# Attention and two expert stages on one core: x in a score bank's columns, k kept, some steps moved

## The chip, the cores and the metric

One NeuronCore of a Trainium2 chip runs the whole program. The metric is the device time of one execution in microseconds (us); lower is better. PE is the matmul engine (PEld its weight loads), DVE the vector engine, ACT the scalar engine, POOL the GpSimd engine, SP the engine whose queue issues most DMAs.

## What is computed

The input of the first stage is q, k, v of 4 batches, 8 heads, 576 rows, 64 columns, all float32. Three stages follow one another:

```python
scores = q @ k^T / 8                        # per batch and head: 576 x 576
kth    = the 32nd largest score of a row
attn   = softmax over the scores >= kth     # the others count as zero
x      = attn @ v                           # put together: 2304 tokens x 512

h = x @ w_in                                # 512 -> 2048
x = (max(h,0) + alpha*min(h,0)) @ w_out     # 2048 -> 512

skip   = x @ w_skip > 0                     # else the row goes out as it is
expert = argmax(x @ w_gate), p its softmax  # 8 experts
out    = x + p * (relu(x @ w1[e]) @ w2[e])  # 512 -> 1024 -> 512
```

Float32 is reached with fp32r matmuls of a high and a low part: three products for each one. The low part is a value less its rounded copy, made by `sub` on POOL (L108).

## The kernel before

**Units and steps.** The unit of attention is one batch, one pair of heads and one tile of 128 query rows. Rows 512 to 575 of both heads make a mixed unit, half as wide. A batch is two works: first the query tiles 0 and 1 of its four pairs (8 units), then the tiles 2, 3 and the mixed one (12 units). There are 80 units. The main loop makes one step per unit, and a step has 14 slots. The list `STEP` says which part of which unit is issued in which slot; `(1, -2, "values")` means: in slot 1, for the unit two steps back. So parts of five units (-2 to 2) are in work at a time, and each engine runs its own instructions in the order in which they were issued.

**A unit's course.** `scores` (PE, L417 and L411) fills four banks of PSUM, `copy` (ACT, L422) brings them to SBUF as `sb`. A step later `fold` (DVE, L438) halves the row by maxima and minima three times; four `round`s find the 32 largest values (MAX8 L447, MATCH_REPLACE8 L450). `exp` (ACT, L472) and `weights` (DVE, L480: compare with the 32nd value, multiply, sum) make the weights, `recip` and `spread` their sum's reciprocal. `turn` (PE, L510 to L516) transposes them, `evac` (ACT, L522 to L533) copies them to `PT` and the reciprocals to `R`. `values` (PE, L539 and L543) multiplies with v, `out` (DVE, L550; ACT, L552; POOL through `sub`) writes the high and the low part of x.

**Heads.** For each pair, `heads` loads q and k, transposes them (PE, L343 and L349) and splits them into parts (`part`: two ACT copies, L330 and L331, and one `sub`). Both works of a batch do that for their own query tiles, and both for all of k. Its pieces are issued by the "heads" entries of `STEP`, for the pair after the current one.

**PSUM.** Eight banks: psS has three (scores, heads, and row tiles at the end), psT two (the fourth score block and transposes 0 and 1 of the weights), psM two (everything of the second and third stages until the end), psX one. psX holds in its two halves, for alternate units, transpose 2 (the tail columns and the reciprocals) and then x of `values`. In the last stage `second` writes its product there too.

**The rest of the work.** Beside attention, a queue `todo` holds the pieces of the second stage (`moe1`: `up` L611, relu L621 to L630, `down` L657, copies L666) with their costs in us; each slot takes as much as its budget allows. Pieces that follow after so many slots go by the list `late`: after the matmuls of an `up` group, `late1` (ACT) runs one slot later, then `LA` slots pass, then `late2` (DVE, L624) reads the bank and frees it; `late3` is POOL's `sub` of g, which `between` holds back from slot 9 on until slot 1 of the next step. At most five or six groups are in this state (`held`). When a work's second stage is done, `rows` issues logits, the routing (`route`, L767 to L776, on DVE), the row tiles (transposed and stored), the ranks (PE, L802 and L803), `slots` (DVE, L812 to L820) and scatters by DMA (POOL, L826).

**The beginning.** In the first 170 us the weights w_in and w_out are converted: 32 loads (SP, L258 and L262), for each three ACT operations (L277 to L281), `bits` (DVE, L285), `split` (POOL, L291 and L108), `store`. `bits` issues the load that stands `AHEAD` places further on.

**The end.** After the last unit the remaining second stage runs, then the experts over blocks of 128 rows (`first` L1015, `second` L1033, `finish` L1041), each beside the splitting of the weights for the next (L986, L987).

`fold` leaves its last instruction in `gate`, and the next `sub` waits for it:

```python
gate[0] = nc.vector.tensor_tensor(o[:, n_], a[:, n_, 0:w], a[:, n_, w:2 * w], op=op)
```

Of the kernel before, what the change touches and what calls it, by code (L numbers as in the profile page):

```python
# [23 lines left out]
STEP = [(0, 0, "exp", 0), (0, 0, "exp", 1), (0, 1, "fold"),  # L24
        (1, -2, "values"), (1, 2, "scores"), (1, 0, "certify"),
        (2, -1, "recip"), (2, 1, "round", 0), (2, 2, "copy", 0),
        (3, 2, "copy", 1),
        (4, 1, "round", 1), (4, 0, "heads", 0),
        (5, -1, "spread"), (5, -1, "turn", 0), (5, 0, "heads", 1),
# [4 lines left out]
        (11, 0, "weights", 1)]  # L34
AHEAD = 3
EC = 32
PH = 9
RD = 3
# [7 lines left out]
CC = 0.5  # L46
LA = 2
CV = 4
HL = 2
# [9 lines left out]
def kernel(  # L59
# [43 lines left out]

    gate, now, held_back = [None], [None], []

# [29 lines left out]

    banks, xbank = [0, 0], [None]

# [17 lines left out]
    def room():  # L155
        return banks[0] - banks[1] < 2
# [78 lines left out]
    wout32 = w_out.bitcast(I32)  # L235
    raws, converted, pads = {}, set(), {}
    todo, late, convq, rowq = [], [], [], []
# [29 lines left out]
    def convert(i):  # L267
# [36 lines left out]

        return none * (CV - 1 if i != 1 else 3 * CV) + [bits] + none * (CV - 1) + [split] + none * CV + [store]


    def heads(b, p, i, us):

        hd = dict(vb=vbd[i], qb=qbd[i])  # L310
        full = [u for u in us if u < SF]
        own = ((full[0], full[-1] + 1), (0, SF))
        nats = {}

        def load():
            tail = att.tile([128, 2, D], F32, name="nat_t", tag="nat_t", bufs=2)
            for s, src in enumerate((q, k)):
                nat = att.tile([128, SF, 2, D], F32, name="nat", tag="nat", bufs=2)
                r0, r1 = own[s]
                for h in range(2):  # L320
                    (nc.scalar if s and quick[0] else nc.sync).dma_start(nat[:, r0:r1, h, :],
                                      src[b, 2 * p + h, 0:SB, :].rearrange("(p r) d -> p r d", p=128)[:, r0:r1])
                (nc.scalar if s and quick[0] else nc.sync).dma_start(tail[s * TL:(s + 1) * TL], src[b, 2 * p:2 * p + 2, SB:S, :].rearrange("h t d -> t h d"))
                nats[s] = nat
            nats[2] = tail
# [8 lines left out]
        def turn(s):  # L334
            if s == 0:

                hd["q"] = att.tile([128, 2, SB], F32R, name="qT", tag="qT", bufs=2)
                hd["k"] = att.tile([128, 2, S + TL], F32R, name="kT", tag="kT", bufs=2)
            r0, r1 = own[s]
            c0, c1 = r0 * 128, r1 * 128  # L340
            pt = htile()[:, c0:c1]
            for r in range(r0, r1):
                nc.tensor.transpose(pt[:, r * 128 - c0:(r + 1) * 128 - c0], nats[s][:, r].rearrange("p h d -> p (h d)"),  # L343
                                    ident)
            late.append((HL, lambda: part(hd["k"][:, :, TL:TL + SB] if s else hd["q"][:, :, c0:c1], pt)))

        def turn_t():
# [3 lines left out]
            def copies():  # L351
                part(hd["k"][:, :, 0:TL], pt[:, TL:128])
                nc.gpsimd.tensor_copy(hd["k"][:, :, S:S + TL], hd["k"][:, :, 0:TL].bitcast(F32))
                if SF not in us:
# [20 lines left out]
        hd["load"] = load  # L375
        return hd, [lambda: turn(0), turn_t, lambda: turn(1)]

# [11 lines left out]
    class Unit:  # L389


        def __init__(self, hd, u, p, getx, col, ai, exact, vi, lastu):
            self.hd, self.u, self.p, self.getx, self.col, self.ai = hd, u, p, getx, col, ai
            self.exact, self.vi, self.lastu = exact, vi, lastu
# [5 lines left out]
        def scores(self):  # L400

            hd, u = self.hd, self.u
            self.sbp, self.sb = padded("sb", 3, 3.0e38)
            self.ps = {}
            for j in range(2):
                for h in range(self.nh):
                    self.ps[h, j] = ptile() if h and j else psS.tile([128, 512], F32, name="ps", tag="ps")
                for i, (a, b_) in enumerate(((0, 0), (1, 0), (0, 1))):
# [5 lines left out]
                    for h in range(2):  # L414
                        gp = slice(h * 64, (h + 1) * 64)
                        c0 = TL * (1 - h) + j * HALF
                        nc.tensor.matmul(self.ps[h, j][:, 0:HALF], lhsT=hd["q"][gp, a, u * 128:(u + 1) * 128],  # L417
                                         rhs=hd["k"][gp, b_, c0:c0 + HALF], **se)
# [74 lines left out]
        def turn(self, h):  # L493
# [5 lines left out]
            if h < 2 and h >= self.nh:  # L499
                return  # L500
            if h < 2:
                pt = ptile()
            else:
                c0 = self.ai % 2 * 256
                pt = xbank[0][:, c0:c0 + 256]
            self.pt[h] = pt
# [28 lines left out]
        def values(self):  # L535
            hd, PT = self.hd, self.PT
            n = 64 if self.mix else 128
            x = self.x = self.pt[2][:, 0:n]
            nc.tensor.matmul(x[:, 0:n], lhsT=hd["vb"], rhs=PT[:, 8, 0:n], start=True, stop=False)  # L539
# [6 lines left out]
        def out(self):  # L546
# [5 lines left out]
            nc.scalar.activation(xh[:, self.p, cols], xf[:, 0:n], AF.Copy)  # L552
            sub(xl[:, self.p, cols], xf[:, 0:n], xh[:, self.p, cols].bitcast(F32))

# [25 lines left out]
    def moe1(xx, cols, x2t, base):  # L580
# [20 lines left out]
        def up(wi, f, sg, half, first):  # L601
# [15 lines left out]

            ra = moe.tile([128, 320], F32, name="ra", tag="ra", bufs=6)[:, 0:n]

# [55 lines left out]
        for hf in range(nhf):  # L675
            for f in range(hf * fs, (hf + 1) * fs):
                for sg, (c0, c1) in enumerate(cols):
                    for half in range(2):
                        one = f % 2 == 0 and sg == 0 and half == 0
                        if half == 0:  # L680
                            parts.append((lambda: room() and held[0] < 6, None))
                        parts.append((6 * (c1 - c0) / 2400, lambda wi=wi, f=f, sg=sg, half=half, one=one:
# [27 lines left out]
    def rows(b, us, colof, x2t, hook, then):  # L710
# [123 lines left out]

        parts = [(lambda: not early[0] and rroom(), None), (0.1, logits)] + [(0, None)] * RD + [(0.1, route)]
        for i in range(nu):
            parts += [(rroom, None), (0.45, lambda i=i: row(i)), (0, None)]
            if i == min(1, nu - 1):
                parts += [(rroom, None), (0.1, ranks)]
# [188 lines left out]
    def second(hs, W):  # L1028
        yp = xtile_()
        i = 0  # L1030
# [74 lines left out]
    def main(work, exact, hooks=(lambda: [], lambda: [])):  # L1105
# [51 lines left out]
        def unit(kx):  # L1157
            if kx not in units:
# [14 lines left out]
                us = work[wi][1]  # L1173
                units[kx] = Unit(hds[pi], u, p, getx, colofs[wi][u], kx, exact, us.index(u), u == us[-1])
            return units[kx]

# [37 lines left out]

        xbank[0] = xtile_()
# [69 lines left out]
        now[0] = None  # L1285
        release(held_back)

    work = []
# [195 lines left out]
```

## Time and profile before

| | us |
|---|---|
| median of 3 runs | 1085.13 (1083.98 to 1085.79) |
| the profiled execution | 1084.56 |
| its span, first to last instruction | 1082.8 |
| PE busy / DVE busy in it | 935.1 / 922.2 |
| ACT busy / POOL busy in it | 703.0 / 429.7 |

The durations come from the one profiled execution, whose span leaves out 1.8 us around it. The mean granted clock of PE is 0.947. In a wait, the idle time of an engine is put down to the instruction that released it last.

### The profile page before, as it was taken

To read this page: it belongs to the slowest core of one execution; us is meant where nothing else is said; L and a number is where in the kernel's file an instruction comes from. 1 tells how busy PE (TensorE), PEld (TensorE's weight loads), DVE (VectorE), ACT (ScalarE), POOL (GpSimd) and SP (SyncE) were. 2 spreads that over 40 slices of the span, in tenths; PEclk is the share of its full clock that TensorE was granted. 3 is DMA by queue.
4 is the path that set the end of the run, shared out by engine and by line. 5 is a ranking of instruction groups with operands and counts; after the bars stand their busy time and mean duration, and the time that the engine had idled before them with its cause. 6 is when DMAs were issued, how large, how long until landed. Compare 5 with 4: busy or idle time off the path is not lost.

```text
span 1082.8 us, 21930 instructions
## 1 busy us (share of the span) xinstructions
PE 935.1 (86%) x7270; PEld 844.8 (78%) x7270; DVE 922.2 (85%) x2943; ACT 703.0 (65%) x1804; POOL 429.7 (40%) x577
## 2 busy tenths in 40 slices
PE   4435668998999989989998998999899998798995
PEld 2224458898998878989998898999789897587884
DVE  4999999999999799999989998999895233899972
ACT  6969857765865576567657766866674343597871
POOL 5766754422542334344224433532341330427221
PEclk9966669998999999999999999999999999899998
DMA  7888985665656566766656666665556798899960
GB/s 218 296 276 214 304 259 184 223 214 172 223 190 229 164 214 195 256 222 225 213 167 215 213 252 224 205 225 195 174 203 235 271 349 340 279 356 397 346 234 15
DMA packets 154282, 254.13 MB, mean 235 GB/s; under 512 B 78062, under 2 KB 110830, under 8 KB 137776
## 3 DMA queue, kind: packets, MB, share of 16 engines
q1 hardware_dynamic: 150464, 247.84, 67.6%
q0 software_dynamic: 2496, 4.50, 1.2%
q8 instruction: 59, 0.97, 0.4%
q14 instruction: 63, 0.52, 0.1%
q10 hardware_dynamic: 1200, 0.30, 0.1%
HBM read 224.20 MB, written 29.71 MB: 234 GB/s over the span
## 4 chain that ended last, share of the span: by engine, by line
PE 41%; DVE 37%; issue 6%; ACT 6%; POOL 5%; DMA 5%; SPq 0%; POOLq 0%; DVEq 0%; ACTq 0%
PE pm L657 14%; DVE v L447 8%; PE pm L611 6%; DVE F L438 5%; DVE Ex L480 5%; DVE m L438 4%; DVE F L450 4%; PE px L1033 4%; PE pm L1015 4%; PE px L543 4%; DVE ra L624 3%; PE ps L417 2%; PE pt L510 2%; POOL cv L108 2%; PE pm L723 1%
## 5 line engine op out<-in xcount | busy, mean ns | idle before, releaser
L611 PE MATMUL pm<-x,wr 128*128 128x256 f32 (+1 forms) x1536 | 248.8, 309 | 17.0 <-DVE ra L624 10.3
L657 PE MATMUL pm<-g,wr 128*128 128x256 f32 (+1 forms) x1536 | 236.0, 304 | 4.1 <-DMA wr<-wout 3.5
L611 PEld LDWEIGHTS pm<-x,wr 128*128 128x128 f32 x1536 | 215.7, 194 | 28.2 <-DVE ra L624 14.8
L657 PEld LDWEIGHTS pm<-g,wr 128*128 128x128 f32 x1536 | 210.2, 190 | 9.9 <-issue 4.1
L447 DVE MAX8 v<-F 128x8 f32<-128x72 f32 (+2 forms) x576 | 212.9, 405 | 0.8
L108 POOL TENSOR_TENSOR g<-ra,g 128x256 fp32r<-128x256 f32 (+1 forms) x128 | 104.9, 824 | 185.8 <-ACT g L630 95.6
L480 DVE SCALAR_TENSOR_TENSOR Ex<-sb,v,Ex 128x577 f32<-128x577 f32 x144 | 129.8, 928 | 0.0
L450 DVE MATCH_REPLACE8 F<-v,F 128x72 f32<-128x72 f32 (+1 forms) x432 | 122.8, 289 | 0.0
L422 ACT ACTIVATE sb<-ps 128x288 f32<-128x288 f32 x224 | 80.0, 411 | 62.2 <-PE ps L417 51.3
L630 ACT ACTIVATE g<-ra 128x256 fp32r<-128x256 f32 (+1 forms) x128 | 57.1, 446 | 75.1 <-DVE ra L624 73.3
L472 ACT ACTIVATE Ex<-sb,st 128x576 f32<-128x576 f32 x144 | 104.7, 775 | 0.1
L522 ACT ACTIVATE PT<-pt 128x512 f32<-128x512 f32 x144 | 86.9, 604 | 16.3 <-PE pt L510 15.6
L624 DVE SCALAR_TENSOR_TENSOR ra<-ra,slope,pm 128x256 f32<-128x256 f32 (+1 forms) x128 | 64.6, 505 | 32.1 <-ACT ra L621 30.2
L543 PE MATMUL px<-PT,vt 128*64 128x128 f32 (+1 forms) x1280 | 89.2, 286 | 0.0
L510 PE MATMUL pt<-ident,Ex 128*128 128x128 f32 x576 | 85.9, 281 | 2.6 <-ACT sb L422 2.6
L108 POOL TENSOR_TENSOR x<-xf,x 128x128 fp32r<-128x128 f32 (+1 forms) x80 | 49.3, 617 | 96.0 <-ACT x L552 94.8
L417 PE MATMUL ps<-kT,qT 64*128 64x288 f32 x576 | 79.5, 348 | 6.1 <-ACT kT L330 2.0
L543 PEld LDWEIGHTS px<-PT,vt 128*64 128x64 f32 x1280 | 70.1, 147 | 9.9 <-issue 1.8
L417 PEld LDWEIGHTS ps<-kT,qT 64*128 64x128 f32 x576 | 61.4, 210 | 19.3 <-issue 9.4
L510 PEld LDWEIGHTS pt<-ident,Ex 128*128 128x128 f32 x576 | 70.7, 146 | 3.9 <-ACT sb L422 3.5
L621 ACT ACTIVATE ra<-pm 128x256 f32<-128x256 f32 (+1 forms) x128 | 52.4, 409 | 30.9 <-PE pm L611 28.7
L438 DVE TENSOR_TENSOR F<-m 128x144 f32<-128x144 f32 (+2 forms) x240 | 70.2, 344 | 0.0
(431 smaller groups left out, 1834.8 us busy)
## 6 DMA issues: line engine op xcount, KB each, us to landing
wr<-win SPq DMA_DIRECT2D x64, 1024.0 KB, 4.9
wr<-wout SPq DMA_DIRECT2D x64, 1024.0 KB, 4.9
wraw<-in_moe_w_dram SPq DMA_DIRECT2D x88, 512.0 KB, 6.3
wr<-in_moe_w_in_dram SPq DMA_DIRECT2D x16, 512.0 KB, 6.1
vt<-in_v_dram SPq DMA_DIRECT2D x32, 256.0 KB, 2.8
win<-cv SPq DMA_DIRECT2D x16, 512.0 KB, 4.8
wr<-in_moe_w_out_dram SPq DMA_DIRECT2D x16, 512.0 KB, 5.6
wout<-cv SPq DMA_DIRECT2D x32, 256.0 KB, 4.1
```

The lines of the kernel that those rows point to most:

```text
L108: i = nc.gpsimd.tensor_tensor(o, a, b, op=OP.subtract)
L417: nc.tensor.matmul(self.ps[h, j][:, 0:HALF], lhsT=hd["q"][gp, a, u * 128:(u + 1) * 128], rhs=hd["k"][gp, b_, c0:c0 + HALF], **se)
L438: gate[0] = nc.vector.tensor_tensor(o[:, n_], a[:, n_, 0:w], a[:, n_, w:2 * w], op=op)
L447: nc.vector.max(v8[:, h, r, :], F[:, h, 0:w])
L450: nc.vector.match_replace(out=F[:, h, 0:w], in_to_replace=v8[:, h, r, :], in_values=F[:, h, 0:w], imm_value=NEG)
L472: nc.scalar.activation(self.Ex[:, h, :], self.sb[:, h, :], AF.Exp, bias=self.st[:, 0, h:h + 1], scale=0.125)
L480: nc.vector.scalar_tensor_tensor(self.Exp[:, cs], self.sbp[:, cs], v8[:, h, 3, 7:8], self.Exp[:, cs], op0=OP.is_ge, op1=OP.mult, accum_out ...
L510: nc.tensor.transpose(pt[:, c * 128:(c + 1) * 128], P[:, c0:c0 + 128], ident)
L543: nc.tensor.matmul(x[h * 64:(h + 1) * 64, 0:n], lhsT=hd["vt"][:, h, c, :], rhs=rhs, start=False, stop=(c == SF - 1))
L611: nc.tensor.matmul(hp[:, 0:n], lhsT=w[:, (f % 2) * 8 + a * 4 + d, :], rhs=x[:, d, c0:c1], start=(i == 0), stop=(i == 3 * KD - 1))
L624: nc.vector.scalar_tensor_tensor(ra, ra, slope[:, f:f + 1], hp[:, 0:n], op0=OP.mult, op1=OP.add)
L657: nc.tensor.matmul(op_[:, 0:n], lhsT=w[:, 2 * f + a, :], rhs=g[(hf + ch) * 8 + f, sg][:, gg, 0:n], start=(i == 0), stop=(i == ni - 1))
```

## The change

- **Kept k.** Only the first work of a batch loads k, transposes it and splits it; the result is kept per pair (four tiles `kT0` to `kT3`), and the second work uses it. q's tile holds two query tiles and not four.
- **Beginning.** Four weight loads are ahead and not three; the fourth is issued behind the second pair's loads. The first conversion's `bits` and `split` come after fewer slots.
- **x in a score bank.** A new part `begin` takes the unit's four score banks. `values` writes x into the columns from 288 on of the bank of the new unit's first head and second half; transpose 2 has psX to itself. Heads' transposes of q and k take banks of psT. `second` takes a bank of psS.
- **Slots.** `values` and `scores` go from slot 1 to slot 2, the copies one slot later each, the first heads entry from slot 4 to slot 3.
- **Low parts.** `sub` of x is kept until slot 1 of the next step (except for a work's last unit). `LA` goes from 2 to 3, with one `ra` buffer less. `route` is issued after the first row tile and three more slots.

The diff, without the parts that only carry these through:

```diff
-        (1, -2, "values"), (1, 2, "scores"), (1, 0, "certify"),
-        (2, -1, "recip"), (2, 1, "round", 0), (2, 2, "copy", 0),
-        (3, 2, "copy", 1),
-        (4, 1, "round", 1), (4, 0, "heads", 0),
+        (1, 0, "certify"),
+        (2, -1, "recip"), (2, 1, "round", 0), (2, 2, "begin"), (2, -2, "values"), (2, 2, "scores"),
+        (3, 2, "copy", 0), (3, 0, "heads", 0),
+        (4, 2, "copy", 1), (4, 1, "round", 1),
...
-AHEAD = 3
+AHEAD = 4
-LA = 2
+LA = 3
...
-        return none * (CV - 1 if i != 1 else 3 * CV) + [bits] + none * (CV - 1) + [split] + none * CV + [store]
+        if i == 0:
+            return none + [bits, split] + none * (2 * CV) + [store]
+        return none * (CV - 1 if i > 1 else 3 * CV) + [bits] + none * (CV - 1) + [split] + none * CV + [store]
...
+        fresh = us[0] == 0
...
+                if s and not fresh:
+                    nc.sync.dma_start(tail[TL:2 * TL], src[b, 2 * p:2 * p + 2, SB:S, :].rearrange("h t d -> t h d"))
+                    continue
...
-                hd["q"] = att.tile([128, 2, SB], F32R, name="qT", tag="qT", bufs=2)
-                hd["k"] = att.tile([128, 2, S + TL], F32R, name="kT", tag="kT", bufs=2)
+                hd["q"], hd["c0"] = att.tile([128, 2, 256], F32R, name="qT", tag="qT", bufs=2), own[0][0] * 128
+                if fresh:
+                    kept[p] = att.tile([128, 2, S + TL], F32R, name="kT", tag=f"kT{p}", bufs=1)
+                hd["k"] = kept[p]
-            pt = htile()[:, c0:c1]
+            pt = ptile()[:, c0:c1]
...
-        return hd, [lambda: turn(0), turn_t, lambda: turn(1)]
+        return hd, [lambda: turn(0), turn_t] + ([lambda: turn(1)] if fresh else [])
...
-                    self.ps[h, j] = ptile() if h and j else psS.tile([128, 512], F32, name="ps", tag="ps")
+                    self.ps[h, j] = ptile() if h and j else htile()
+            spare[0] = self.ps[0, 1]
...
-            if h < 2:
-                pt = ptile()
-            else:
-                c0 = self.ai % 2 * 256
-                pt = xbank[0][:, c0:c0 + 256]
+            pt = ptile() if h < 2 else xtile_()
...
-            x = self.x = self.pt[2][:, 0:n]
+            bank = spare[0] if spare[0] is not None else htile()
+            spare[0] = None
+            x = self.x = bank[:, HALF:HALF + n]
...
-            sub(xl[:, self.p, cols], xf[:, 0:n], xh[:, self.p, cols].bitcast(F32))
+            def low():
+                sub(xl[:, self.p, cols], xf[:, 0:n], xh[:, self.p, cols].bitcast(F32))
+            if self.end or now[0] is None:
+                low()
+            else:
+                held_x.append(low)
...
-            ra = moe.tile([128, 320], F32, name="ra", tag="ra", bufs=6)[:, 0:n]
+            ra = moe.tile([128, 320], F32, name="ra", tag="ra", bufs=5)[:, 0:n]
-                            parts.append((lambda: room() and held[0] < 6, None))
+                            parts.append((lambda: room() and held[0] < 5, None))
...
-        parts = [(lambda: not early[0] and rroom(), None), (0.1, logits)] + [(0, None)] * RD + [(0.1, route)]
+        parts = [(lambda: not early[0] and rroom(), None), (0.1, logits)] + [(0, None)] * RD
         for i in range(nu):
+            if i == 1:
+                parts += [(0, None)] * RD + [(0.1, route)]
             parts += [(rroom, None), (0.45, lambda i=i: row(i)), (0, None)]
...
-        yp = xtile_()
+        yp = htile()
...
-            for i in range(AHEAD):
+            for i in range(AHEAD - 1):
...
+        if not exact:
+            conv_load(*convs[AHEAD - 1])
...
                 if x == 1 or now[0] is None:
                     release(held_back)
+                    release(held_x)
```

## Rows read from the trace of the kernel before

**Rows 1.** The page: engine shares; DVE and clock in 40 slices.

```profile
PE 935.1 (86%) x7270; PEld 844.8 (78%) x7270; DVE 922.2 (85%) x2943; ACT 703.0 (65%) x1804; POOL 429.7 (40%) x577
...
PE   4435668998999989989998998999899998798995
...
DVE  4999999999999799999989998999895233899972
```

**Rows 2.** Stretches of 25 us: busy us per engine, granted clock, DMA share, GB/s.

```profile
225.00:250.00 25.00, 25.00 (x248) 23.74 (x247) 24.83 (x93) 17.02 (x54) 6.55 (x13) 1.00 0.73 250
250.00:275.00 25.00, 21.95 (x167) 20.71 (x166) 22.10 (x95) 15.10 (x44) 7.76 (x14) 0.80 0.50 157
```

**Rows 3.** DVE's waits, 175 to 825 us: total us, times, longest us.

```profile
DVE ra L624 <- ACT ra L621: 8.5, 13, 2.3
DVE rc L767 <- ACT lg L732: 8.3, 3, 3.8
DVE rc L767 <- ACT lg L730: 5.3, 2, 2.7
DVE xf L550 <- PE px L543: 3.6, 3, 1.3
DVE tot L814 <- PE pm L803: 3.1, 4, 1.1
```

**Rows 4.** DVE's waits, 0 to 175 us.

```profile
DVE cv L285 <- ACT cv L281: 14.6, 7, 7.3
DVE ra L624 <- ACT ra L621: 3.5, 2, 2.7
```

**Rows 5.** Timeline, 20 to 30 us: start, us, engine, line, idle before.

```profile
24.38 0.91 DVE L285 SCALAR_TENSOR_TENSOR cv<-cv 128x512 int32<-128x512 int32 x1 [2.67 <-ACT cv L281]
...
27.60 0.67 ACT L277 ACTIVATE cv<-wr 128x512 f32<-128x512 f32 x1 [3.25 <-DMA wr<-in_moe_w_in_dram]
...
29.60 1.13 DVE L285 SCALAR_TENSOR_TENSOR cv<-cv 128x512 int32<-128x512 int32 x1 [0.71 <-ACT cv L281]
```

**Rows 6.** PE's waits, 175 to 825 us.

```profile
PE pm L611 <- DVE ra L624: 10.3, 18, 1.4
PE px L539 <- ACT R L528: 7.6, 6, 1.8
PE px L512 <- DVE xf L550: 6.7, 8, 3.0
...
PE ps L343 <- ACT sb L422: 1.3, 2, 0.9
```

**Rows 7.** Groups by shape, 175 to 825 us: busy us, mean ns, idle before.

```profile
L480 DVE SCALAR_TENSOR_TENSOR Ex<-sb,v,Ex 128x577 f32<-128x577 f32 x121 | 106.2, 904 | 0.0
...
L108 POOL TENSOR_TENSOR x<-xf,x 128x128 fp32r<-128x128 f32 x53 | 34.1, 643 | 61.3 <-ACT x L552 60.8
```

**Rows 8.** Timeline around 519 us.

```profile
519.08 0.80 DVE L480 SCALAR_TENSOR_TENSOR Ex<-sb,v,Ex 128x577 f32<-128x577 f32 x1
...
519.48 0.73 POOL L108 TENSOR_TENSOR x<-xf,x 128x128 fp32r<-128x128 f32 x1 [0.26 <-ACT x L552]
...
519.81 1.02 DVE L480 SCALAR_TENSOR_TENSOR Ex<-sb,v,Ex 128x577 f32<-128x577 f32 x1
```

**Rows 9.** Groups by shape again, 175 to 825 us: k's splitting.

```profile
L330 ACT ACTIVATE kT<-ps 128x512 fp32r<-128x512 f32 x25 | 15.0, 598 | 7.4 <-PE ps L343 7.4
...
L108 POOL TENSOR_TENSOR kT<-raw__6693,kT 128x512 fp32r<-128x512 f32 x1 | 1.3, 1290 | 0.1
```

**Rows 10.** Timeline around 544 us: scores, x's reader, score copies.

```profile
544.07 0.79 PE L417 MATMUL ps<-kT,qT 64*128 64x288 f32 x7
...
544.28 0.29 DVE L550 TENSOR_TENSOR xf<-px,R 128x128 f32<-128x128 f32 x1 [1.25 <-PE px L543]
...
544.77 1.02 ACT L422 ACTIVATE sb<-ps 128x288 f32<-128x288 f32 x3 [1.40 <-PE ps L417]
```

**Rows 11.** PE's waits, 825 to 1083 us.

```profile
PE px L1033 <- DVE orow L1041: 2.3, 1, 2.3
```

More of the change, by code (lines that the diff above doesn't have):

```diff
@@ L102 @@
     ctx.enter_context(tc.manual_schedule())
-    gate, now, held_back = [None], [None], []
+    gate, now, held_back, held_x = [None], [None], [], []
     def sub(o, a, b):
@@ L134, in xtile_ @@
         return psX.tile([128, 512], F32, name="px", tag="px")
-    banks, xbank = [0, 0], [None]
+    banks, spare = [0, 0], [None]
     def mtile():
@@ L235 @@
     wout32 = w_out.bitcast(I32)
-    raws, converted, pads = {}, set(), {}
+    raws, converted, pads, kept = {}, set(), {}, {}
     todo, late, convq, rowq = [], [], [], []
@@ L312, in heads @@
         own = ((full[0], full[-1] + 1), (0, SF))
+        fresh = us[0] == 0
+        assert own[0][1] - own[0][0] <= 2
         nats = {}
@@ L344, in turn @@
                                     ident)
-            late.append((HL, lambda: part(hd["k"][:, :, TL:TL + SB] if s else hd["q"][:, :, c0:c1], pt)))
+            late.append((HL, lambda: part(hd["k"][:, :, TL:TL + SB] if s else hd["q"][:, :, 0:c1 - c0], pt)))
         def turn_t():
@@ L351, in copies @@
             def copies():
-                part(hd["k"][:, :, 0:TL], pt[:, TL:128])
-                nc.gpsimd.tensor_copy(hd["k"][:, :, S:S + TL], hd["k"][:, :, 0:TL].bitcast(F32))
+                if fresh:
+                    part(hd["k"][:, :, 0:TL], pt[:, TL:128])
+                    nc.gpsimd.tensor_copy(hd["k"][:, :, S:S + TL], hd["k"][:, :, 0:TL].bitcast(F32))
                 if SF not in us:
@@ L393, in __init__ @@
             self.hd, self.u, self.p, self.getx, self.col, self.ai = hd, u, p, getx, col, ai
-            self.exact, self.vi, self.lastu = exact, vi, lastu
+            self.exact, self.vi, self.lastu, self.end = exact, vi, lastu, False
             self.mix = u == SF
@@ L398, in __init__, with begin @@
             self.pt = {}
-        def scores(self):
-            hd, u = self.hd, self.u
+        def begin(self):
             self.sbp, self.sb = padded("sb", 3, 3.0e38)
@@ L406, in scores @@
                 for h in range(self.nh):
-                    self.ps[h, j] = ptile() if h and j else psS.tile([128, 512], F32, name="ps", tag="ps")
+                    self.ps[h, j] = ptile() if h and j else htile()
+            spare[0] = self.ps[0, 1]
+        def scores(self):
+            hd, u = self.hd, self.u
+            for j in range(2):
                 for i, (a, b_) in enumerate(((0, 0), (1, 0), (0, 1))):
@@ L416, in scores @@
                         c0 = TL * (1 - h) + j * HALF
-                        nc.tensor.matmul(self.ps[h, j][:, 0:HALF], lhsT=hd["q"][gp, a, u * 128:(u + 1) * 128],
+                        nc.tensor.matmul(self.ps[h, j][:, 0:HALF], lhsT=hd["q"][gp, a, u * 128 - hd["c0"]:(u + 1) * 128 - hd["c0"]],
                                          rhs=hd["k"][gp, b_, c0:c0 + HALF], **se)
@@ L1174, in unit @@
                 units[kx] = Unit(hds[pi], u, p, getx, colofs[wi][u], kx, exact, us.index(u), u == us[-1])
+                units[kx].end = last[wi] == kx
             return units[kx]
@@ L1213, in queue_moe @@
             todo.extend(parts)
-        xbank[0] = xtile_()
         padded("sb", 3, 3.0e38)
@@ L1286, in main @@
         release(held_back)
+        release(held_x)
     work = []
```

## The prediction

> **What bounds the kernel now.** I read the page's engine shares first. PE is busy for 86% of the span and DVE for 85%, and the slices show both near 9 tenths from the seventh slice to the thirty-first [rows 1]; neither alone explains 1082.8 us. The table of 25 us stretches is next: from about 175 to 825 us there are stretches with both engines full (24.83 of 25 us on DVE, 25.00 on PE), and between them stretches like 250 to 275 us, where DVE has 22.10 us, PE 21.95 us and the granted clock is 0.80 [rows 2]. PE's records overlap and their ends are modelled, so its 25.00 is an upper bound of its work. DVE's durations hardly overlap, so a full DVE is the firmer limit. I then asked what DVE waits for: in the 650 us of the middle 13.6 us go to the routing's logits, 8.5 us to relu outputs, 3.6 us to x, 3.1 us to rank sums [rows 3]; in the first 175 us, 14.6 us go to converted weights [rows 4]. The rest of DVE's time is work, part of it stretched by POOL. Last, I read what PE waits for in the middle [rows 6] and late [rows 11]. So the middle is bound by DVE's queue, with PE close behind: a saving on DVE counts until PE is full, and a new PE wait counts where PE is full already.
>
> A slot's length: 121 mask multiplications in 650 us [rows 7], two to a full unit, make 60.5 full units of 10.7 us; with 14 slots that is 0.77 us a slot.
>
> **x's low parts.** The subtraction on POOL, 53 times 643 ns for full units, now starts behind ACT's copy of x, where DVE multiplies weights with the mask [rows 7, 8]. Such a multiplication took 0.80 us before POOL's subtraction began and 1.02 us across it [rows 8]. Over all of them the mean is 904 ns, thus 121 x 0.104 = 12.6 us of stretching [rows 7]. Held until slot 1, the subtraction goes behind the fold, beside the rounds. Not all 12.6 us is x's (other subtractions fall there too), while some of the first 175 us is to be added. I take -11 us, bounds -13 and -2. Behind it on POOL's queue wait only the certificate and later g parts, each 0.62 us later.
>
> The Trainium skill (SBUF — State Buffer, Who interferes with whom) says that the port pair is an exclusive lock, and that the loser blocks for the whole instruction. By it each multiplication met by a subtraction would lose up to 0.64 us, an estimate of 34 us for 53; the 1.02 us row shows a third of that, and the row decides.
>
> **Routing.** Its first DVE reduction waits for the logits five times, 13.6 us, longest 3.8 us [rows 3]. It moves behind the first row tile and three more slots, about four slots or 3.1 us of other DVE work; PE, which is late there, gets that time. Of 13.6 us I count 11 gone. Against it, the rank matmuls now stand one slot behind routing, not two, so PE may wait for DVE and then DVE for PE: today's 3.1 us [rows 3] can grow by a slot for each of some seven works (5.4 us); I take 2. Scatters, which are DMAs of POOL's queue, and the row of x2 that feeds the next stage go later by the same slots; in the middle nobody waits for them soon. Net -9 us, bounds -13 and -3.
>
> **Relu's reader.** One slot later on DVE. The 13 waits of 8.5 us [rows 3] are 0.65 us each, less than a slot, and some 3.5 us stand in the start [rows 4]. I take -7. The matmul bank is held a slot longer: PE waits for that reader 18 times already, 10.3 us [rows 6], at most 18 x 0.77 = 14 us more on PE; as PE mostly has slack there I take +2. Net -5, bounds -9 and +5. That one ra buffer goes costs nothing: with a group every 3 to 4 slots five are not held at once.
>
> **Values and banks.** Today values and the transposes of unit tails share one bank. PE waits 7.6 us for ACT to empty R and 6.7 us for DVE to read x, though x and the new transposes lie in different halves [rows 6]. Both go: values use columns 288 on of a score bank, and the tail bank is empty ten slots earlier. PE waits are worth little where DVE is full: -3 us, bounds -8 and 0. But x comes a slot later (0.77 us), and its score matmuls stand behind it in the same bank. After a unit with one head, DVE comes early and waits today, 1.25 us before 544.28 [rows 10]. If x is freed only with the scores, that is their 0.79 us and more on top. About four units of each of three batches have so little slack: 12 x 0.4 = +5 us, bounds +1 (slot only, four waits) and +9 (ACT's copies of 1.02 us as well [rows 10]). The value loads on SP that follow values are a slot later, for a pair two pairs away: nothing. Scores and copies are a slot later, ten slots ahead of their fold: nothing.
>
> The Trainium skill (PSUM — Partial Sum Buffer, PSUM bank collisions raise a hardware error) wants accesses guarded by bank, whatever the columns. The wait of PE for x in another half agrees with it [rows 6]. It would make this term nearer +9 than +1, since ACT and DVE now read one bank; no row of before shows two readers ordered so.
>
> Transposes of heads move to the two other banks (psT), a slot earlier. Their old wait for score copies, 1.3 us [rows 6], goes. In 12 steps of a batch (two for each of four first pairs, one for each of four second pairs), psT then holds the fourth score block, heads, and both transposes of weights: PE's first weight transpose waits for ACT's score copies (1.02 us for three [rows 10]), the second for the heads' two copies (0.60 us each [rows 9]). In between PE has two to three slots of matmuls. +4 us, bounds 0 and +10.
>
> **Kept k.** Each of 16 second pairs loses four k transposes, ACT copies of 2 x 598 ns, POOL's subtraction of k (1.29 us [rows 9]), the same for the tail in small, and its k loads on SP. That is over 16 x 1.2 = 19 us of ACT and 16 x 1.29 = 21 us of POOL, but ACT (65%) and POOL (40%) don't bound [rows 1]. What counts is less stretching of DVE and four transposes of PE each: -3, bounds -8 (a third of the 21 us, as in [rows 8], and a little PE) and 0.
>
> **Beginning and end.** With a fourth weight load ahead, ACT waits less for DMA (3.25 us at 27 us), and DVE's gaps of 2.67 and 0.71 us behind ACT [rows 5] go: -3.4, bounds -5 and 0; the first 7.3 us [rows 4] stay, nothing is there to do. From 47 us DVE is full anyway, and earlier bits add no work. In the last stage the output product gets a psS bank and not the single one: the 2.3 us that PE waits for the row's reader [rows 11] lie on the ending chain: -2, bounds -2.3 and 0.
>
> **Sum.** -11 -9 -5 -3 +5 +4 -3 -3.4 -2 = -27.4 us. Where PE is full (about a third of the middle, the down stages, [rows 2]) savings on DVE don't count: a third of 11 + 5 + 3 is 6.3 us back. -21.1 us from the profiled execution's 1084.56 us (span 1082.8; median of the runs 1085.13) gives 1063.5 us. Late next: PE in the down stages.
>
> **Rivals.**
> 1. PE takes over. DVE runs further ahead and waits at x and relu instead; then only a third of x, relu and k counts (-6) with routing -5, start and end -5, against +9 of psT and x: -7, or 1077. For it: both engines are at 25 of 25 us [rows 2]. Against it: in the relu (up) stages PE is the one that waits for DVE [rows 6].
> 2. The loose ends all close: upper bounds of x, routing and relu (-35), start and end -7, k and values -10, +6 of new waits: -46, thus 1039. It needs PE to have slack in the down stages, against its 25.00 us.
> 3. Slower: psT. If in the 12 steps of a batch PE's transposes wait for ACT, the time is lost on PE, and weights' copies, values and x follow. All gains (some 31 us without this term) are used up from 31/48 = 0.65 us a step on. At 0.9 us, ACT's three score copies less a slot's matmuls, that is 48 x 0.9 = 43 against 31: 1096. A PE that pauses also lost its clock, as at 250 us with 0.80 [rows 2]. Against it: ACT waits for PE rather than lags, at 544.77 with the scores just done [rows 10].
> 4. It does not do what it says: x stays tied to score copies, and low parts meet the fold's next stage; gains and costs cancel within 2.2 us.
>
> **How the numbers follow.** Forecast (1045 to 1072) 0.58; rival 1 (1072 to 1082.9) 0.20; rival 2 below 1045 0.07; rival 4 0.05; rival 3 above 1087.3 0.10. About 0.2%, 2.2 us, is what a measurement here can tell from no change. Faster 0.85, same 0.05, slower 0.10. Range 1045 to 1081: it leaves out 0.07 below and some 0.13 above.
>
> **What would show it.** Right: waits of DVE for lg nearly gone; mask multiplications near 0.82 us in the mean; no PE wait for R or x before the tail transposes; heads' k copies halved; DVE's gaps at 24 and 29 us gone. Wrong: long PE waits before weight transposes for ACT's sb or kT copies; DVE waits for px or ra above today's 12 us; PE waits for ra well over 20 us; dips of the clock at more places than before.

## The result and the profile after

The change takes 1071.83 us (median of 4 runs, 1070.96 to 1073.94) against 1085.46 us before: a ratio of 0.9875, 95% interval 0.9851 to 0.9899, or 13.6 us less. 1063.5 us was forecast, within 1045 to 1081 us. The direction and the range held. Of the parts, few came out as worked: kept k, priced at 3 us, gave the most, and three moves (routing and relu's reader, priced as gains, and the later slot, priced at a few us of loss) cost 6 to 9 us each.

The page after: engine shares, and the slices of PE and DVE, as in [rows 1].

```profile
PE 934.3 (87%) x7206; PEld 840.5 (79%) x7206; DVE 909.7 (85%) x2943; ACT 681.4 (64%) x1740; POOL 379.1 (35%) x529
...
PE   4456488999999889899989998999899898898995
...
DVE  5999999999998999899879998998994333799872
```

DVE has 12.5 us less work, ACT 21.6 and POOL 50.6; PE has the same. The next two tables cut both kernels at the same places of the program: where DVE takes the 11th and the 79th reciprocal of the units (one reciprocal to a unit). The columns are the stretch, its length, then busy us of PE, PEld, DVE, ACT and POOL, the granted clock, DMA. Before:

```profile
0.00:170.80 170.80, 89.48 (x540) 70.43 (x541) 149.44 (x415) 128.60 (x303) 110.69 (x137) 0.78 0.84 258
170.80:826.50 655.70, 618.30 (x5438) 576.26 (x5439) 620.01 (x2281) 437.16 (x1296) 245.41 (x376) 0.98 0.63 209
826.50:1082.80 256.30, 227.31 (x1296) 198.16 (x1296) 152.78 (x250) 137.27 (x205) 73.56 (x66) 0.96 0.77 286
```

After:

```profile
0.00:157.30 157.30, 86.54 (x519) 66.79 (x521) 144.78 (x414) 124.44 (x291) 100.41 (x126) 0.83 0.88 272
157.30:813.60 656.30, 617.80 (x5400) 574.01 (x5397) 611.26 (x2281) 420.46 (x1244) 205.38 (x338) 0.98 0.62 204
813.60:1070.50 256.90, 230.00 (x1294) 199.73 (x1292) 153.68 (x250) 136.49 (x205) 73.34 (x66) 0.95 0.78 285
```

The whole gain of these two executions stands in the first stretch: 13.5 us, of which 4.7 us are DVE's work (149.44 to 144.78) and 8.8 us its idle time (21.4 to 12.5). In the middle, DVE's work falls by 8.7 us (620.01 to 611.26), and its idle time grows by 9.4 us (655.70 - 620.01 = 35.7 to 45.0): nothing is left. The end is as long as before.

What DVE waits for in the middle after, from 175 to 815 us, against [rows 3] (us in total, times, longest):

```profile
DVE xf L563 <- ACT sb L437: 22.5, 15, 3.0
DVE ra L644 <- ACT ra L641: 7.9, 11, 1.7
DVE rc L804 <- ACT rt L793: 5.3, 5, 1.8
DVE xf L563 <- issue: 3.3, 2, 2.2
DVE tot L834 <- PE pm L823: 1.5, 3, 0.8
```

The 13.6 us for the logits are gone. In their place x's reader waits 22.5 us for ACT's score copies, which it never did before, and the second half of the routing waits 5.3 us for ACT. PE's waits in the same window, against [rows 6]:

```profile
PE pm L631 <- DVE ra L644: 15.6, 17, 1.8
PE pm L822 <- ACT xr L767: 5.8, 4, 2.0
PE pm L762 <- DVE rt L835: 4.3, 3, 2.0
PE pt L521 <- ACT sb L437: 4.0, 7, 0.9
```

R and x's reader are no longer among them. The wait for relu's reader grew from 10.3 to 15.6 us, and 10.1 us before the ranks (L822) and the next row tile (L762) are new. One of x's waits, from the timeline after; before, the same unit waited 1.25 us [rows 10]:

```profile
524.61 1.09 PE L556 MATMUL ps<-PT,vt 128*64 128x128 f32 x16
525.63 0.79 PE L432 MATMUL ps<-kT,qT 64*128 64x288 f32 x7
...
526.33 1.02 ACT L437 ACTIVATE sb<-ps 128x288 f32<-128x288 f32 x3 [0.95 <-PE ps L432]
...
527.45 0.29 DVE L563 TENSOR_TENSOR xf<-ps,R 128x128 f32<-128x128 f32 x1 [2.96 <-ACT sb L437]
```

x is complete at 525.7 us; DVE starts to read it at 527.45 us, when the third copy, out of the same bank, has ended at 527.35 us.

### The profile page after: what moved, and what is told of

It is laid out like the page before. It is cut to its first block, busy times and chain, and to the rows that moved or that the text cites. A ratio compares the mean times of both kernels' runs of the same rounds, so it can differ in the third digit from the quotient of the medians.

```text
span 1070.5 us, 21725 instructions
## 1 busy us (share of the span) xinstructions
PE 934.3 (87%) x7206; PEld 840.5 (79%) x7206; DVE 909.7 (85%) x2943; ACT 681.4 (64%) x1740; POOL 379.1 (35%) x529
## 4 chain that ended last, share of the span: by engine, by line
PE 50%; DVE 29%; ACT 5%; DMA 4%; issue 4%; POOL 1%; SPq 0%; POOLq 0%; DVEq 0%; ACTq 0%
PE pm L677 18%; PE pm L631 7%; DVE v L462 6%; PE ps L556 5%; DVE Ex L495 5%; PE ps L1055 4%; PE pm L1037 4%; DVE F L453 4%; PE ps L432 3%; DVE F L465 3%; PE pt L521 3%; DVE ra L644 3%; DVE m L453 3%; DMA wr<-wout 2%; ACT sb L437 1%
## 5 line engine op out<-in xcount | busy, mean ns | idle before, releaser
L631 PE MATMUL pm<-x,wr 128*128 128x256 f32 (+1 forms) x1536 | 246.2, 310 | 22.2 <-DVE ra L644 16.8
L677 PE MATMUL pm<-g,wr 128*128 128x256 f32 (+1 forms) x1536 | 233.6, 302 | 6.6 <-DVE ra L644 2.3
L108 POOL TENSOR_TENSOR g<-ra,g 128x256 fp32r<-128x256 f32 (+1 forms) x128 | 108.2, 848 | 220.5 <-ACT g L650 114.0
L521 PE MATMUL pt<-ident,Ex 128*128 128x128 f32 x576 | 91.0, 291 | 18.0 <-ACT sb L437 16.2
L108 POOL TENSOR_TENSOR x<-xf,x 128x128 fp32r<-128x128 f32 (+1 forms) x80 | 36.7, 458 | 173.5 <-DVE st L500 141.4
L556 PE MATMUL ps<-PT,vt 128*64 128x128 f32 (+1 forms) x1280 | 90.5, 289 | 0.0
L556 PEld LDWEIGHTS ps<-PT,vt 128*64 128x64 f32 x1280 | 71.3, 150 | 10.1 <-issue 2.5
L453 DVE TENSOR_TENSOR F<-m 128x144 f32<-128x144 f32 (+2 forms) x240 | 67.2, 332 | 0.0
```

Source lines behind the costliest of these rows:

```text
L108: i = nc.gpsimd.tensor_tensor(o, a, b, op=OP.subtract)
L521: nc.tensor.transpose(pt[:, c * 128:(c + 1) * 128], P[:, c0:c0 + 128], ident)
L556: nc.tensor.matmul(x[h * 64:(h + 1) * 64, 0:n], lhsT=hd["vt"][:, h, c, :], rhs=rhs, start=False, stop=(c == SF - 1))
L631: nc.tensor.matmul(hp[:, 0:n], lhsT=w[:, (f % 2) * 8 + a * 4 + d, :], rhs=x[:, d, c0:c1], start=(i == 0), stop=(i == 3 * KD - 1))
L677: nc.tensor.matmul(op_[:, 0:n], lhsT=w[:, 2 * f + a, :], rhs=g[(hf + ch) * 8 + f, sg][:, gg, 0:n], start=(i == 0), stop=(i == ni - 1))
```

## Experiments

All ratios are to the kernel before on the same chip, five rounds or more each, with 95% intervals. The kernel before took 1086.1 to 1089.3 us beside them, and the expected times were written for one of 1085.5 us, so it is the ratio times 1085.5 us that compares with an expectation. What a part is worth is a difference of two ratios, and such a price is good to about 3 us either way.

### Kept k and the beginning alone

The kernel before with the `kept`, `fresh`, `AHEAD` and first-conversion lines of the change, and `ra` with five buffers for room.

> The kernel before with two parts alone: k kept per pair (with q's smaller tile and one ra buffer less, which make room for it), and the beginning. By the prediction's terms (-3 and -3.4) 1078 to 1080 us. By the traces, where the twentieth unit starts 14.4 us earlier than before and only part of that can be other parts: 1074 to 1078 us. If k's ACT and POOL time counts for more in the middle than thought, the middle gains 4 us or more here as well.

1065.92 us, ratio 0.9792 (0.9769 to 0.9815). That is 22.7 us below before, beyond what the two readings with a time expected, and faster than the whole change. The third reading, a middle that gains 4 us or more, came. Its first two stretches, cut as above:

```profile
0.00:162.40 162.40, 86.69 (x525) 67.31 (x526) 149.19 (x414) 124.38 (x291) 100.72 (x128) 0.79 0.86 265
162.40:807.80 645.40, 612.19 (x5389) 569.97 (x5389) 612.63 (x2281) 421.60 (x1244) 213.96 (x337) 0.99 0.61 207
```

8.4 us come from the first stretch, nearly all of it idle time of DVE (21.4 to 13.2 us). In the middle DVE has 7.4 us less work than before, and here its idle time does not grow (35.7 to 32.8 us), so the middle keeps 10.3 us. Everything else in the change is thus worth a loss of some 9 us (0.9875 against 0.9792).

### k in both works

```diff
-        fresh = us[0] == 0
+        fresh = True
```

> As the change, but the second work of a batch loads, transposes and splits k again. By the prediction's term kept k is worth 3 us: 1073 to 1077 us. By the runs so far (k and the beginning alone gave 22.7 us, the beginning is worth about 7): 15 us, 1084 to 1090 us, with its loss spread over the second works' stretches, from 140 us on, and DVE's folds stretched again.

1087.25 us, ratio 1.0009 (0.9994 to 1.0023): without kept k the change gives nothing. k is worth 0.0134, or 14.5 us, as the second reading had it, and not 3. The middle of this run:

```profile
163.34:828.98 665.64, 625.57 (x5454) 579.53 (x5449) 618.88 (x2282) 437.05 (x1296) 244.33 (x377) 0.98 0.62 206
```

DVE's work is back by 7.6 us, with no DVE instruction added; its idle time is 46.8 us, 1.7 more. Another 6 us are lost in the first stretch (163.3 against 157.3 us), 2.8 us of them between the tenth and the eleventh reciprocal, early in the second work of the first batch (150.5 to 163.3 us, against 147.2 to 157.3). PE is busy there throughout in both (12.82 of 12.84 us, 9.97 of 10.08), with 107 matmuls for 95 and a granted clock of 0.85 for 0.94.

### The beginning as before

```diff
-AHEAD = 4
+AHEAD = 3
...
-        if i == 0:
-            return none + [bits, split] + none * (2 * CV) + [store]
```

(and four lines of its issue)

> As the change, but the beginning as before it: three weight loads ahead, the first conversion's steps at their old distance. Forecast term 3.4 us: 1074 to 1077 us, DVE's gaps at 24 and 29 us back, all units 2 to 4 us later from the start. If later steps of the conversion gain from the fourth load as well (the tenth unit starts 9.8 us earlier with everything): 1078 to 1083 us.

1081.58 us, ratio 0.9939 (0.9917 to 0.9962). The beginning is worth 0.0064, or 6.9 us, more than the forecast's 3.4, though with 3.6 us either way hardly beyond it. In the profiled runs 3.7 us of that are in the first stretch (160.99 against 157.30 us). They are there at the first unit's reciprocal (47.4 against 43.7 us) and stay the same to the eleventh, so the second reading, by which later steps of the conversion gain as well, is not borne out. DVE's waits for converted weights in this stretch, with the old beginning and with the change:

```profile
DVE cv L285 <- ACT cv L281: 14.5, 6, 7.7
```

```profile
DVE cv L285 <- ACT cv L281: 8.7, 2, 7.5
```

All of them end within the first 38 us. The rest of the 6.9 us came in the middle and the end, where the edit has nothing, and with one profile of each that split is not firm.

### Low parts at once

```diff
-            if self.end or now[0] is None:
+            if True:
                 low()
```

> As the change, but x's low part is subtracted at once, as before the change. By the prediction's largest term it was worth 11 us: 1080 to 1084 us. By the trace after, where the mask multiplications are as long as before and only the folds are shorter (some 6 us), and the beginning gained some 5 us beyond kept k and the beginning: 1076 to 1080 us. If neither lies on the path: 1070 to 1073 us.

1082.81 us, ratio 0.9947 (0.9933 to 0.9960), which is 1079.7 us beside a kernel before of 1085.5 us and lies in the second reading. Holding is worth 0.0072, 7.8 us, within the change. The profiled run took 1087.29 us, 4.5 us above the median, so its idle time is rather too long. The middle:

```profile
159.37:827.23 667.86, 626.22 (x5400) 581.33 (x5397) 617.03 (x2282) 420.72 (x1244) 224.28 (x337) 0.96 0.59 200
```

DVE's work grows by 5.8 us there and its idle time to 50.8 us. Most of the work is not where the prediction looked for it: about 2 us are in the mask multiplications and 4 us in the fold's two first instructions. Mask multiplications and one of these folds from 165 to 800 us (mean in ns), before, then after, then with low parts at once:

```profile
L480 DVE SCALAR_TENSOR_TENSOR Ex<-sb,v,Ex 128x577 f32<-128x577 f32 x116 | 102.6, 911 | 0.0
L438 DVE TENSOR_TENSOR F<-sb 128x576 f32<-128x576 f32 x51 | 43.4, 852 | 0.0
```

```profile
L495 DVE SCALAR_TENSOR_TENSOR Ex<-sb,v,Ex 128x577 f32<-128x577 f32 x116 | 101.8, 906 | 0.0
...
L453 DVE TENSOR_TENSOR F<-sb 128x576 f32<-128x576 f32 x52 | 40.7, 783 | 0.0
```

```profile
L495 DVE SCALAR_TENSOR_TENSOR Ex<-sb,v,Ex 128x577 f32<-128x577 f32 x115 | 103.1, 924 | 0.0
...
L453 DVE TENSOR_TENSOR F<-sb 128x576 f32<-128x576 f32 x50 | 40.7, 815 | 0.0
```

The multiplication stays at 906 ns after the change: what x's subtraction left there, other subtractions of g and of heads filled. Of the 11.4 us by which the multiplications of the middle exceed 0.809 us each before, 5.1 us are in those that meet a subtraction of x (1.0 us where they meet nothing else); after, it is 2.8 of 11.2 us, and those that meet only heads or g went from 6.3 to 8.4 us.

### Low parts with k and the beginning alone

The first experiment, and `held_x` as in the change.

> The kernel before with kept k, the beginning and the held low parts alone; heads stay in psS and a slot later, x in psX. If low parts are worth here what they are worth within the change (7 to 8 us): 1056 to 1060 us, a ratio near 0.972. If most of that was the untangling of the change's other moves: 1063 to 1067 us. Against the run with x besides in psX it shows what heads' banks are worth.

1062.92 us, ratio 0.9782 (0.9754 to 0.9810), against 0.9792 without. The intervals overlap: held low parts gain 1 us there, with some 4 us either way, between the two readings. In the one profile of each, the two first stretches are 6.8 us shorter and the end is 3.8 us longer, which is not firm. So the 7.8 us above are hardly a price of this edit by itself; that within the change it takes away what the other moves make worse is argued and not shown.

### Relu's reader two slots behind

```diff
-LA = 3
+LA = 2
```

> As the change, but relu's reader runs two and not three slots behind relu. Theory C' (the matmul bank held a slot longer makes PE late: its waits for the reader are 15.6 us, 10.3 before): undone they return to 10 to 12 us and the time falls to 1066 to 1070 us. Theory D (a slot more spares DVE waits, 5 us net as forecast): DVE's waits for relu grow from 8 to 12 us or more, 1074 to 1078 us.

1065.93 us, ratio 0.9793 (0.9780 to 0.9806): the later reader cost 0.0082, 8.9 us, as theory C' had it and somewhat more. Its middle and PE's wait there:

```profile
158.60:809.43 650.83, 613.45 (x5392) 570.43 (x5389) 610.20 (x2281) 423.26 (x1244) 198.74 (x338) 0.98 0.60 205
```

```profile
PE pm L631 <- DVE ra L644: 10.8, 13, 1.6
```

DVE's own waits for relu grow as theory D had it (7.9 to 14.9 us), yet DVE's idle time falls from 45.0 to 40.6 us: PE has its bank back a slot sooner, and x's reader waits less for the score copies behind PE's matmuls (16.2 us, 22.5 with the change).

### Routing early

```diff
-        ... + [(0, None)] * RD
+        ... + [(0, None)] * RD + [(0.1, route)]
         for i in range(nu):
-            if i == 1:
-                parts += [(0, None)] * RD + [(0.1, route)]
```

> As the change, but routing stands ahead of the first row tile again. Theory C (routing's move cost the middle: ranks stand one slot behind it, PE waits 5.8 us for ACT's row tiles before the ranks and 4.3 us behind them, DVE 5.3 us for ACT's exponential, and PE's clock falls to 1.2 GHz at more boundaries): undone it brings 1071.8 down to 1064 to 1069 us, though DVE's waits for logits come back with some 12 us. Theory D (the move is the gain of 9 us that was forecast): 1077 to 1083 us.

1070.48 us, ratio 0.9815 (0.9795 to 0.9835), below the change's 0.9875: the later routing cost 0.0060, 6.5 us, within theory C. DVE's waits for logits come back with 6.3 us, half of what theory C had. Its account of PE is not borne out: the 10.1 us at the ranks and the next row tile fall to 3.5 us, but 4.9 us before `up` take their place, and all of PE's waits for row tiles' copies and routing results go only from 10.8 to 8.4 us. The profiled run of this kernel (1076.22 us) is slower than its median, so its stretches are not read further, and where the 6.5 us lie stays open.

### Begin, values and scores in slot 1

```diff
+        (1, 2, "begin"), (1, -2, "values"), (1, 2, "scores"), (1, 0, "certify"),
+        (2, -1, "recip"), (2, 1, "round", 0), (2, 2, "copy", 0),
+        (3, 2, "copy", 1), (3, 0, "heads", 0),
+        (4, 1, "round", 1),
```

> As the change, but begin, values and scores stand in slot 1 and the copies in slots 2 and 3, as before the change. Theory A: x's product and the copies that hold it back come one slot (0.77 us) earlier against DVE, so x's waits fall by about 15 x 0.7 = 10 us; PE's wait for PT grows by some us: 1062 to 1068 us. Theory B (the order on PE counts, not the slot): within 3 us of 1071.8 us.

1069.22 us, ratio 0.9810 (0.9788 to 0.9832): the later slot cost 0.0065, 7.1 us. x's reader still waits 20.9 us for score copies, so the time did not come by that wait, as theory A had it. By the ratio it is 1064.8 us, within theory A's times and below B's.

### x in halves of psX

```diff
-            bank = spare[0] if spare[0] is not None else htile()
-            spare[0] = None
-            x = self.x = bank[:, HALF:HALF + n]
+            x = self.x = self.pt[2][:, 0:n]
```

(with transpose 2 in alternate halves of one bank again)

> As the change, but x and the tail transposes share psX in halves, as before the change; slots, kept k, beginning, low parts, relu's reader and routing stay. Theory A: DVE's waits for ACT's score copies before x vanish (26 us to 4 to 8 us, the rest for PE's own product), PE's waits for R and for x's reader come back with some 14 us, mostly hidden: 1060 to 1067 us. Theory B: DVE's gain is taken by PE's waits, 1071 to 1078 us.

1074.84 us, ratio 0.9870 (0.9845 to 0.9896), the same as the change. DVE's waits in the middle:

```profile
DVE ra L646 <- ACT ra L643: 22.2, 17, 3.7
DVE xf L565 <- PE px L558: 10.6, 7, 2.7
```

The 22.5 us for score copies are gone, and relu's waits went from 7.9 to 22.2 us. Theory A falls. As theory B had it, the wait in the score bank shows that PE is late; taken away, DVE meets the next thing that PE owes (10.6 us for PE's product of x are new as well).

### x in the bank that is copied first

```diff
-            spare[0] = self.ps[0, 1]
+            spare[0] = self.ps[0, 0]
```

(this bank taken last of the three of psS)

> As the change, but x stands in the bank of the score block that ACT copies first (first head, first half; this bank is taken last of the three), not in the one copied third. Theory A (x's reader on DVE waits for ACT's copy out of the same bank, 22.5 us in 15 waits plus 3.3 us put down to nothing, and that ate the middle's gain): the reader is free about 1.2 us earlier at each wait, two copies and some matmuls; its waits fall from 26 us to 8 to 12 us, and the time from 1071.8 to 1058 to 1064 us. Theory B (PE is late there anyway, the wait only shows it): waits move to px or relu, 1069 to 1073 us.

1082.25 us, ratio 0.9936 (0.9911 to 0.9961), slower than the change, which neither theory had. x's reader does start earlier behind its scores, right after the first copy:

```profile
528.53 1.02 ACT L437 ACTIVATE sb<-ps 128x288 f32<-128x288 f32 x3 [0.95 <-PE ps L432]
...
529.04 0.29 DVE L563 TENSOR_TENSOR xf<-ps,R 128x128 f32<-128x128 f32 x1 [2.74 <-ACT sb L437]
```

but the wait there is 2.74 us for 2.96, since DVE came 0.4 us earlier against the copies. DVE, ACT and POOL run the same instructions in the same order as with the change, and PE the same matmuls; x's waits fall only from 22.5 to 19.7 us, those for relu grow from 7.9 to 14.0 us, and the middle is 6.2 us longer, with a mean clock of 0.97 for 0.98. Why a shorter wait made the middle longer stays open.

### The three moves undone together, and x's bank besides

The three diffs above (relu's reader, routing, slots) at once:

> As the change, but the three moves that cost time one by one are undone together: relu's reader two slots behind, routing ahead of the row tiles, begin, values, scores and copies in their old slots. Kept k, the beginning, the held low parts, x in the score bank and heads in psT stay. If the three costs add (9, 6.5 and 7 us): 1050 to 1056 us, a ratio near 0.967 to the kernel before. If they have one cause in common (each gives the same few us of slack between PE and DVE): 1060 to 1065 us.

And with x in halves of psX:

> As the run with the three moves undone, and x besides in psX's halves as before. Theory A (x's reader waiting for ACT's score copies costs time once nothing else hides it): 5 to 12 us below that run. Theory B (PE is late there, and psX's halves cost PE waits for x's reader of 10 us instead): within 3 us of it.

1061.52 us, ratio 0.9770 (0.9744 to 0.9795), and 1062.59 us, ratio 0.9778 (0.9752 to 0.9804). The three costs (0.0082, 0.0060, 0.0065) give 0.0105 together, half of their sum, as the second reading had it: they overlap, which speaks for a cause in common without naming it. The bank makes no difference here either. The second of the two runs and the one with k, the beginning and low parts (0.9782) differ by the banks of heads' transposes, their slot and the bank of `second`: together these are worth nothing that can be measured. The two middles:

```profile
159.15:803.94 644.79, 611.87 (x5395) 570.58 (x5395) 608.08 (x2280) 424.19 (x1244) 201.44 (x338) 0.98 0.62 207
```

```profile
159.24:802.34 643.10, 609.33 (x5389) 566.23 (x5389) 607.80 (x2281) 424.82 (x1244) 203.19 (x338) 0.99 0.62 208
```

DVE's work is 3 us below the change's, its idle time 36.7 and 35.3 us instead of 45.0: the idle time of before (35.7), with 12 us less of DVE's work. These two, the first experiment, the one with low parts and relu's reader two slots behind lie within 0.9770 to 0.9793; all five beat both kernels, and the simplest is kept k with the beginning alone.

## Why the prediction came out as it did

That the total came out near the forecast was luck. Kept k and the beginning, 6.4 us in the sum, gave 22.7 us by themselves. The rest, about -15 us in the sum with its discount, cost some 9 us.

**Kept k** was mis-sized: 3 us forecast with bounds to 8, 14.5 us measured. ACT's work left out was counted about right: 19 us forecast, 16.6 us between the middles with k twice and with the change (437.05 to 420.46). POOL's was not: 21 us forecast, for the large subtractions alone, 39.0 us measured there (244.33 to 205.38). The step that failed is "What counts is less stretching of DVE and four transposes of PE each". The stretching by itself came to the bound: DVE's work fell by 7.4 us in the middle (first experiment) and by 7.6 us (k twice), with the same instructions. It lies at k's own operations: by an estimate from starts and ends in the traces, DVE's instructions with two inputs that meet an operation of POOL on k exceed the like ones that meet nothing by 13.6 us in the middle before, and by 4.1 us in the first experiment; the others exceed them by some 14 and 16 us. What the sum had nothing for is the first stretch, 6.0 us, where the second work begins, and 1.7 us of idle time in the middle. Which of k's matmuls, copies and subtractions cost these was not separated.

**The beginning** went the forecast way, 6.9 for 3.4 us, and the 3.7 us that the traces place are near the forecast. The gap of 0.71 us at 29 us is gone and that of 2.67 us is 1.23 us [rows 5]; with the old beginning, the change had further waits of 1.0 to 1.5 us at 15, 31 and 38 us.

**Low parts** were the largest term, 11 us, read from the mask multiplications. In the change they are worth 7.8 us, with k and the beginning alone about 1 us. The failed step is the reading of [rows 8]. The subtraction of x runs there from 519.48 to 520.21 us, so it began inside the multiplication that took 0.80 us, and cost it nothing. The next one began 0.40 us before the subtraction's end and took 0.21 us more. How much a multiplication loses hangs on which of the two began first, as rows with a subtraction of g, from the same trace, show more strongly:

```profile
475.58 0.81 DVE L480 SCALAR_TENSOR_TENSOR Ex<-sb,v,Ex 128x577 f32<-128x577 f32 x1
...
476.25 0.88 POOL L108 TENSOR_TENSOR g<-ra,g 128x320 fp32r<-128x320 f32 x1 [0.94 <-ACT g L630]
...
476.32 1.42 DVE L480 SCALAR_TENSOR_TENSOR Ex<-sb,v,Ex 128x577 f32<-128x577 f32 x1
```

The subtraction began 0.07 us ahead and still had 0.81 us to go; the multiplication lost 0.61 us. So [rows 8] shows no stretch by a third, and it does not speak against the lock that the prediction set aside by it. In the middle before, 17 of the 53 subtractions of x began inside a multiplication and were the longer ones (0.53 to 1.08 us), while more than half of the multiplications' extra time lies in those that meet no subtraction of x. The mean of 904 ns [rows 7] was put down to the one subtraction that the timeline showed; holding it left the mean where it was, and the sign that the prediction gave, 0.82 us, did not come.

**Routing**, forecast -9 us, cost 6.5. The wait itself went as read, 13.6 us to none. The bounds failed: the price of a rank matmul one slot behind routing was bounded by DVE's wait, 5.4 us. In the change 10.1 us of waits stand on PE and 5.3 us on DVE behind ACT's exponential, which now comes after a row tile's copy; undone, the latter is 1.0 us, but PE's waits of this kind only move. So the size is shown and its place is not.

**Relu's reader**, -5 us, cost 8.9, beyond the bound of +5. The bound priced PE's later bank at "mostly slack". Rival 1 named this: DVE runs further ahead and waits elsewhere. It had 1077 us for the whole change, and its mechanism came: idle time of DVE grew by 9.4 us as its work fell by 8.7. That the total came out 5 us better is due to k and the beginning, not to the middle.

**Values and banks.** That x's reader is held by the bank was foreseen as a price (+5, to +9); 25.8 us of waits appeared. The Trainium skill (PSUM — Partial Sum Buffer, PSUM bank collisions raise a hardware error) wants two readers of one bank kept apart. The program keeps to that, as the trace shows: x is read at 527.45 us, 0.10 us behind the copy; no run here lets the two meet. But the run with x in halves gives the same time, so the 25.8 us are no cost by themselves. The cost is in the slot, 7.1 us, for which the prediction had a lower bound of 1 us (0.77 us a slot, four waits). The slot itself was taken too long: a mixed unit has one multiplication and takes 14 slots as well, and 68 units in 655.7 us make 0.69 us a slot; that moves no term by much.

**psT**, rival 3: PE's waits before the weights' transposes came to 4.0 us, the forecast 4, and nowhere near 0.65 us a step; the two runs that differ by it show no cost. **The end**, -2 us, gave nothing: PE's wait of 2.3 us [rows 11] is gone and the stretch is still 256.9 us (256.3).

So the sum of 21.1 us was near 13.6 by terms that erred both ways. In the middle the discount of a third for a full PE failed: even the whole of it would have made the moved readers worth nothing, and they cost time, which the sum had no term for. The runs fit one account: DVE's waits there are the shadow of PE's lateness, and moving a reader past one wait puts it before the next; three such moves together gave a loss of 0.0105. That is argued from where the waits went. What did count were k, which takes work off the queues, and the loads ahead.

What stays open: which of PE's pauses makes it late. The longer the idle time of DVE in a middle, the lower in general its granted clock (0.99 with 32.8 and 35.3 us, 0.97 with 48.5, 0.96 with 50.8), but 0.98 goes with 35.7 us before and 47.3 with x in halves of psX, and no run held the clock fixed. Which is cause and which is effect was not separated.

## What to carry to other kernels

When two engines are both near full and feed each other, idle time of one behind a semaphore is no saving in waiting: ask what the releaser is late with, and price the move by the releaser's queue. Work that is taken out of a queue, also of an engine at 40%, was worth more than any reordering here; about half of that is instructions of the engine that bounds, which no longer wait behind it. Before a longer instruction is put down to a neighbour, compare their starts over the whole trace and not in one row. Undo the parts of a bundle one by one and then together: the parts that gained alone were faster than the bundle, and prices that were measured inside it did not add.

## What the runs showed of the hardware

A DVE instruction with two inputs from SBUF and a subtraction or cast of POOL hold each other up, and the one that began first loses nothing. In the middle before, 46 of the 122 mask multiplications meet no subtraction or cast of POOL and take 809 ns in the median; the 23 that meet one which began later take 809 ns as well (792 to 821). The 13 that meet one which began earlier, with 0.2 us or more to go, are longer by what is left of it less 0.190 to 0.194 us. The other 40 meet several, or one that is nearly over. The fold's first instruction does the same with some 0.13 us in place of 0.19. MAX8 over 576 columns, with one input, takes 744 ns in the median where it meets none and at most 753 ns where it meets one that began earlier. The other way, the 17 subtractions of x that began inside a multiplication all end 0.31 to 0.33 us behind its end and take up to 1.08 us, where the 25 that meet no such instruction take 0.45 to 0.47 us.

Leaving out k's subtractions changed DVE's busy time in the middle by 7.4 and 7.6 us in two pairs of runs, with the same number of DVE instructions but for one at the edge of the stretch. Holding x's alone left the mean of the mask multiplication at 906 ns, from 911 ns, since other subtractions met it instead.
